# Earlier weight loads, later q and k loads and an earlier U product in a fused attention and mixer kernel

## The chip, the cores and the metric

The kernel runs on one core of a Trainium2 chip. Its time is the device time of one execution in microseconds (us). A core has five engines with an instruction stream each: PE (TensorE, matmuls; its weight loads are shown apart as PEld), DVE (VectorE), ACT (ScalarE), POOL (GpSimd) and SP (SyncE, which here only issues DMAs). Each engine takes its instructions in order. SP and POOL issue DMAs: SP's go to a hardware queue, POOL's to a software queue, and the same 16 DMA engines move both.

## The reference

Batch 4, 8 heads, 768 positions, head size 64; x is then 4 x 768 x 512.

```
scores = q @ k^T / 8 + bias          # bias: -slope_h * distance
keep   = (column < 8) or (0 <= row - column < 96)
a      = softmax(scores where keep)  # others -1e9
x      = (a @ v), heads side by side # (4, 768, 512)
h      = x^T @ U @ V                 # U 768x32, V 32x768: mixes positions
u      = x + h^T
out    = u + relu(u @ w_ch1) @ w_ch2 # 512 -> 2048 -> 512
```

The mask leaves each block of 128 rows its own block of columns, the block before it, and the first 8 columns.

## The kernel before, in words

**Pairs.** The work goes by pairs of heads: pair i is batch i // 4, heads 2 (i % 4) and the next. There are 16. `NP` is 4 and `NPE` is 8. For a pair the steps are: `load_qk` and `load_v` (SP issues the loads of q, k and v in float32), `cast_qk` and `cast_v` (casts to float16, on POOL from pair 3 on), then the turning of q and k, which for pairs below 8 is PE transposes (`st_T`) and for pairs 8 to 15 two DMA transposes that SP issues (`turn`, L323 for k, L326 for q). `st_K` (L335, L336, DVE) or `st_KA` (L290, L291, POOL) makes `kA`, the keys of the block before with the 8 global ones. `st_A` makes `vA` the same way, as a POOL copy (L299) below pair 8 and as DMAs from pair 8 on (L302, L303). `st_S` computes scores on PE (L360, L367) and drains them on DVE with the bias (L392); `st_E` is the exponential on ACT (L404). `st_V` is the product with v on PE (L416, L420); DVE divides (L425, L439) and POOL casts the result to float16 (L440) as `x16`.

**The mixer.** For each pair, `st_M1` multiplies x16 by U on PE (L449; batch 0: L457), DVE copies the result (L453), `st_MT` turns it on PE (L466, drained by L467), `st_M3` multiplies by V (L503) and DVE adds it to x (L508); POOL casts u to float16 (L512), and `st_X` has SP issue a DMA transpose of it (L492), which makes `uT`. Batch 0 uses `st_M2` instead.

**The feed-forward.** It is cut into units: an up unit is 8 matmuls with w1 (L609) and a Relu on ACT (L614); a down unit is 4 matmuls with w2 (L639) and, in the last groups, 8 matmuls with sums of quarters (L659). `fill(n)` runs n units from two queues, so units stand between the attention steps of the pairs as filler for PE. A batch's units are queued (`queue_ff`) when its four pairs are done.

**Weights.** w1 is loaded in four quarters of 512 columns and w2 in four pieces of 512 rows, each by one DMA that POOL issues (`load_w1` L222, `load_w2` L225), which casts to float16 on the way (512 KB written each).

**Order.** All of it is written out by hand: nothing reorders it, and an engine runs its instructions in the order of the program. First comes a loop over pairs 0 to 3, then a stretch that finishes batch 0, then a loop in which iteration i does the attention of pair i, the product with v and the mixer of pair i - 1 and the loads for later pairs. Staging buffers for q and k are two deep.

Of the kernel before, what the change touches and what calls it, by code (L numbers as in the profile page):

```python
# [20 lines left out]
def kernel(  # L21
# [24 lines left out]
    NP = H // 2  # L46
    NPE = 2 * NP
# [38 lines left out]
    def ps_cps(name):  # L86
        return psum.tile([P, 512], FP32, name=name, tag="cps", bufs=2)
# [8 lines left out]
    def load_qk(i, behind=None):  # L96

        b, h0 = i // NP, 2 * (i % NP)
        got = []
        for src, nm in ((q, "qst"), (k, "kst")):  # L100
            st = stp.tile([P, 2, NSB, D], FP32, name=nm, tag=nm, bufs=2)
            if behind is not None:
                behind.memset(st[0:1, 0, 0, 0:1], 0.0)
            if i < NPE:
                nc.sync.dma_start(  # L105
                    st.rearrange("p h n d -> p h (n d)"),
                    src[b, h0:h0 + 2].rearrange("h (p n) d -> p h (n d)", n=NSB),
                )
            else:
                nc.sync.dma_start(  # L110
                    st.rearrange("p h n d -> p (h n) d"),
                    src[b, h0:h0 + 2].rearrange("h (n p) d -> p (h n) d", p=P),
                )
            got.append(st)
        staged[i] = got

    def cast_qk(i, *engs):
        got = []
        for st, nm, eng in zip(staged.pop(i), ("q16", "k16"), engs * 2):
            st16 = stp.tile([P, NSB, 2, D], FP16, name=nm, tag=nm, bufs=2)  # L120
            turn_over = eng.copy if eng is nc.scalar else eng.tensor_copy
            turn_over(st16.rearrange("p n h d -> p h n d"), st)
            got.append(st16)
        cast[i] = got
# [17 lines left out]
    NPAIR = B * NP  # L142
# [77 lines left out]
    def load_w1(c):  # L220
        js = slice(c * (DFF // 4), (c + 1) * (DFF // 4))
        nc.gpsimd.dma_start(w1_16[:, :, js], w1v[:, :, js])  # L222

    def load_w2(c):
        nc.gpsimd.dma_start(w2_16[:, 4 * c:4 * c + 4], w2v[:, 4 * c:4 * c + 4])  # L225
# [85 lines left out]
    def st_P(i):  # L311
        nc.vector.tensor_copy(  # L312
            vas[i][0:NG, 1:].rearrange("p n h d -> p n (h d)"),
            vts[i][0:NG, 0:1].rearrange("p n h d -> p n (h d)").broadcast_to(
                (NG, NSB - 2, 2 * (D + 1))
            ),
        )
# [84 lines left out]
    def st_E(i, hi):  # L402
        ep = scp.tile([P, W], FP16, name=f"ep{hi}", tag=f"ep{hi}")
        nc.scalar.activation(  # L404
            ep, sps.pop((i, hi)), AF.Exp, scale=slope[2 * (i % NP) + hi]
        )
        eps[i, hi] = ep

    def st_V(i, hi):
        b, h = i // NP, 2 * (i % NP) + hi  # L410
        ep, vt, vA = eps.pop((i, hi)), vts[i], vas[i]
        obf = ps_cps("ob") if (i, hi) == (NP - 1, 1) else ps_ob()
        ob = obf[:, 0:NSB * (D + 1)].rearrange("p (n d) -> p n d", n=NSB)
        for qi in range(NSB):
            if qi:
                nc.tensor.matmul(  # L416
                    ob[:, qi], ep[:, OF[qi - 1]:OF[qi - 1] + P], vA[:, qi - 1, hi],
                    start=True, stop=False,
                )
            nc.tensor.matmul(  # L420
                ob[:, qi], ep[:, DG[qi]:DG[qi] + P], vt[:, qi, hi],
                start=(qi == 0), stop=True,
            )
        rcp = vap.tile([P, NSB], FP32, name="rcp", tag="rcp")
        nc.vector.reciprocal(rcp, ob[:, :, D])  # L425
        xo = xs[b][:, :, h * D:(h + 1) * D]
        x16 = x16s[b][:, i % NP, :, hi * D:(hi + 1) * D]
        rb = rcp.unsqueeze(2).broadcast_to((P, NSB, D))
        if i == NP - 1:
            if hi == 1:  # L430
                nc.vector.tensor_tensor(x16, ob[:, :, 0:D], rb, ALU.mult)
            else:
                for n in range(NSB):
                    nc.scalar.activation(
                        x16[:, n], ob[:, n, 0:D], AF.Copy, scale=rcp[:, n:n + 1]
                    )
            later.append((xo, ob[:, :, 0:D], rb))
            return
        nc.vector.tensor_tensor(xo, ob[:, :, 0:D], rb, ALU.mult)  # L439
        nc.gpsimd.tensor_copy(x16, xo)  # L440
# [22 lines left out]
    def st_MT(i):  # L463
        b, dc = i // NP, i % NP
        tps = ps_ob()
        nc.tensor.matmul(tps[:, 0:P], turn16[i % 2], ident16, start=True, stop=True)  # L466
        nc.vector.tensor_copy(tmps[b][:, dc * P:(dc + 1) * P], tps[:, 0:P])  # L467
# [22 lines left out]
    def st_X(i):  # L490
        b, dc = i // NP, i % NP
        nc.sync.dma_start_transpose(  # L492
            uTs[b][:, dc].rearrange("d (n p) -> d n p", n=NSB),
            x16s[b][:, dc].rearrange("p n d -> p (n d)"),
        )
# [195 lines left out]
    def fill(n):  # L691
        for _ in range(n):
            unit()
            if jobs:
                jobs.popleft()()
# [22 lines left out]
    for i in range(NP):  # L718
        st_SE(i, 0)
        if i:  # L720
            st_V(i - 1, 0)
        cast_v(i)
        st_A(i)
        if i < 2:
            load_v(i + 2)
        if i == 0:
            load_uv()
        if i == 1:
            load_qk(NP)
        if i == 2:  # L730
            load_w1(0)
            load_qk(NP + 1, nc.gpsimd)
        if i == 3:
            load_v(NP)
        if i == NP - 1:
            st_M1(i - 2)
        if i:
            st_T(i + 1)
        st_SE(i, 1)
        if i == 2:  # L740
            st_M1(i - 2)
        if i:
            st_V(i - 1, 1)
        else:
            st_T(i + 1)
        st_KA(i + 1, nc.vector)
        st_P(i)
        if i == 0:
            cast_qk(i + 2, nc.vector)
        elif i < 3:  # L750
            cast_qk(i + 2, nc.gpsimd)
        if i == 2:
            load_w1(1)
        st_SE(i, 2)
        if i >= 2:
            st_M2(i - 2)
# [17 lines left out]
    for i in range(NP, NPAIR + 2):  # L774
        b, hp = divmod(i, NP)
        live = i < NPAIR
        units = iter(
            (1, 1, 1, 1, 1, 1, 1, 1, 0) if i + 1 < NPE
            else (1, 1, 1, 2, 1, 1, 1, 1, 1) if i < 2 * NP + 1
            else (2, 1, 1, 2, 1, 1, 1, 1, 1)  # L780
        )
        held[0] = i < NP + 3
        if hp == 0 and live and b + 1 < B:
            new_batch(b + 1)
        if live and i > NP:
            st_S(i, 0)
        if NPE <= i + 1 < NPAIR:
            turn(i + 1)
        if i + 1 < NPAIR:
            load_v(i + 1)  # L790
        if i + 2 < NPE:
            load_qk(i + 2)
        fill(next(units))
        if NP < i <= NPAIR:
            st_V(i - 1, 0)
        if i + 1 < NPE:
            st_T(i + 1)
        if i == NP:
            load_w1(2)
        if live:  # L800
            cast_v(i)
            st_A(i)
            if i == NP:
                load_w1(3)
        fill(next(units))
        if live:
            st_S(i, 1)
        fill(next(units))
        if NP < i <= NPAIR:
            st_V(i - 1, 1)  # L810
        if NPE <= i + 3 < NPAIR:
            load_qk(i + 3)
        if i > NP + 1 and (i - 2) % NP == NP - 1:
            queue_ff((i - 2) // NP)
            ahead[0] = 1
        if i == NPAIR + 1:
            break
        fill(next(units))
        if live:
            st_S(i, 2)  # L820
            if i < NPE:
                st_P(i)
        fill(next(units))
        if i > NP:
            st_M1(i - 1)
        if i == NP + 1:
            load_w2(0)
            load_w2(1)
        if i + 2 < NPE:
            cast_qk(i + 2, nc.gpsimd)  # L830
        if live:
            st_E(i, 0)
        fill(next(units))
        if i > NP:
            st_MT(i - 1)
        if NPE <= i + 1 < NPAIR:
            st_K(i + 1)
        fill(next(units))
        if i > NP:
            st_M3(i - 1, 0)  # L840
        if live:
            st_E(i, 1)
        fill(next(units))
        if i > NP:
            st_M3(i - 1, 1)
            st_X(i - 1)
        if i == NP + 1:
            load_w2(2)
            load_w2(3)
        if NPE <= i + 2 < NPAIR:  # L850
            cast_qk(i + 2, nc.gpsimd)
        fill(next(units))
# [38 lines left out]
```

## Time and profile before

| what | value |
|---|---|
| median of 3 runs | 233.44 us (232.91 to 236.33) |
| the profiled execution: its own time | 232.94 us |
| its span in the profile | 231.0 us |
| PE busy | 223.2 us, 97% of the span |
| DVE, ACT, POOL busy | 152.7, 110.9, 80.5 us |
| granted TensorE clock | 1.0 throughout |
| DMA | 36.66 MB, mean 159 GB/s; the share of the 16 engines is about 0.9 to 1.25 in most stages from 24 to 108 us and below 0.8 afterwards |
| w1 and w2 loads | 8 of 512 KB, median 8.9 us from issue to landing |
| q and k loads | 16 of 384 KB each, median 4.2 and 4.9 us to landing |

The span runs from the first to the last instruction of the program; the 1.9 us beside it lie around the program. The profile's durations are those of one execution. PE's busy time counts matmuls as pipelined, so it is not a measure of how well each is used; what it shows here is where PE has gaps.

### The profile page before, as it was taken

To read this page: it belongs to the slowest core of one execution; us is meant where nothing else is said; L and a number is where in the kernel's file an instruction comes from. 1 tells how busy PE (TensorE), PEld (TensorE's weight loads), DVE (VectorE), ACT (ScalarE), POOL (GpSimd) and SP (SyncE) were. 2 spreads that over 40 slices of the span, in tenths; PEclk is the share of its full clock that TensorE was granted. 3 is DMA by queue.
4 is the path that set the end of the run, shared out by engine and by line. 5 is a ranking of instruction groups with operands and counts; after the bars stand their busy time and mean duration, and the time that the engine had idled before them with its cause. 6 is when DMAs were issued, how large, how long until landed. Compare 5 with 4: busy or idle time off the path is not lost.

```text
span 231.0 us, 5678 instructions
## 1 busy us (share of the span) xinstructions
PE 223.2 (97%) x2324; PEld 161.8 (70%) x2324; DVE 152.7 (66%) x350; ACT 110.9 (48%) x167; POOL 80.5 (35%) x131
## 2 busy tenths in 40 slices
PE   7989999999999999999999999999999999999994
PEld 2455678788644457766666656866688888888883
DVE  3697797868677667566656675779895524444452
ACT  6776957685621313827363707473633334333320
POOL 6399728577444243433424051504120100000000
PEclk9999999999999999999999999999999999999999
DMA  6997998999999999897786955633131302011112
GB/s 183 321 280 201 280 203 188 261 259 175 213 210 244 209 315 216 220 182 188 157 226 134 258 140 145 148 100 79 32 81 48 79 3 91 1 48 45 45 48 91
DMA packets 86561, 36.66 MB, mean 159 GB/s; under 512 B 74152, under 2 KB 83592, under 8 KB 86536
## 3 DMA queue, kind: packets, MB, share of 16 engines
q1 hardware_dynamic: 81480, 32.01, 55.1%
q0 software_dynamic: 5056, 4.29, 12.3%
q8 instruction: 18, 0.29, 0.5%
q14 instruction: 7, 0.06, 0.1%
HBM read 27.46 MB, written 6.29 MB: 146 GB/s over the span
## 4 chain that ended last, share of the span: by engine, by line
PE 86%; POOL 3%; DMA 3%; ACT 3%; DVE 2%; issue 1%; SPq 1%; POOLq 0%
PE hps L609 35%; PE cps L639 22%; PE cx L659 8%; PE cy L659 5%; PE sc L360 4%; DMA vst<-in_v_dram 3%; PE ob L420 2%; PE ob L416 2%; PE sc L367 2%; ACT htr L614 1%; ACT ep L404 1%; PE tp L250 1%; PE sc L503 1%; PE ob L503 1%; SPq L105 1%
## 5 line engine op out<-in xcount | busy, mean ns | idle before, releaser
L614 ACT ACTIVATE htr<-hps 128x512 f16<-128x512 f32 x96 | 56.6, 598 | 85.0 <-PE hps L609 82.2
L609 PE MATMUL hps<-uT,w 128*128 128x256 f16 x756 | 96.2, 273 | 0.5 <-DVE uT L485 0.3
L609 PEld LDWEIGHTS <-w 128*128 128x128 f16 x756 | 70.5, 98 | 11.3 <-issue 0.4
L639 PE MATMUL cps<-w,htr 128*128 128x512 f16 x224 | 56.9, 379 | 0.0
L392 DVE SCALAR_TENSOR_TENSOR sp<-sc,relcat 128x512 f32<-128x512 f32 (+1 forms) x72 | 43.3, 641 | 15.5 <-PE sc L360 8.9
L404 ACT ACTIVATE ep<-sp 128x1408 f16<-128x1408 f32 x24 | 32.8, 1374 | 16.3 <-DVE sp L392 16.3
L512 POOL CAST x<-x_sb 128x768 f16<-128x768 f32 x12 | 10.3, 856 | 60.5 <-DVE x_sb L508 60.5
L639 PEld LDWEIGHTS <-htr 128*128 128x128 f16 x224 | 19.1, 97 | 16.6
L440 POOL CAST x<-x_sb 128x384 f16<-128x384 f32 x30 | 15.8, 525 | 26.8 <-DVE x_sb L439 26.7
L360 PEld LDWEIGHTS <-kT 64*128 64x128 f16 x192 | 8.2, 93 | 15.1 <-issue 13.5
L540 DVE TENSOR_TENSOR s<-htr 128x512 f16<-128x512 f16 x20 | 9.3, 464 | 12.7 <-ACT htr L614 12.7
L439 DVE TENSOR_TENSOR x_sb<-ob,rcp 128x384 f32<-128x384 f32 x30 | 16.7, 558 | 1.0
L659 PEld LDWEIGHTS <-s 128*128 128x128 f16 x160 | 15.5, 98 | 1.8
L360 PE MATMUL sc<-qT,kT 64*128 64x128 f16 x192 | 16.7, 221 | 0.0
L420 PE MATMUL ob<-v,ep 128*128 128x65 f16 x192 | 16.2, 193 | 0.0
L420 PEld LDWEIGHTS <-ep 128*128 128x128 f16 x192 | 13.8, 98 | 2.7 <-ACT ep L379 0.3
L664 DVE TENSOR_TENSOR x_sb<-cx,x_sb 128x256 f32<-128x256 f32 x20 | 8.5, 423 | 10.1 <-PE cx L659 10.0
L136 POOL CAST v<-vst 128x768 f16<-128x768 f32 x16 | 13.4, 839 | 4.5 <-DMA vst<-in_v_dram 4.5
L367 PE MATMUL sc<-qT,kA 64*128 64x128 f16 x160 | 14.1, 216 | 0.9 <-DVE kA L286 0.9
L379 ACT ACTIVATE ep<-sc 128x512 f16<-128x512 f32 (+1 forms) x24 | 12.0, 559 | 5.1 <-PE sc L367 4.8
L416 PE MATMUL ob<-vA,ep 128*128 128x65 f16 x160 | 14.3, 194 | 0.2 <-DVE vA L312 0.2
L659 PEld LDWEIGHTS <-htr 128*128 128x128 f16 x120 | 11.7, 98 | 1.3
(102 smaller groups left out, 269.4 us busy)
## 6 DMA issues: line engine op xcount, KB each, us to landing
qst<-in_q_dram SPq DMA_DIRECT2D x16, 384.0 KB, 4.2
kst<-in_k_dram SPq DMA_DIRECT2D x16, 384.0 KB, 4.9
vst<-in_v_dram SPq DMA_DIRECT2D x16, 384.0 KB, 3.4
out_dram<-x_sb SPq DMA_DIRECT2D x23, 256.0 KB, 2.3
w<-in_moe_w_ch_dram POOLq DMA_DIRECT2D x8, 512.0 KB, 8.9
vA<-v SPq DMA_DIRECT2D x8, 152.3 KB, 4.3
out_dram<-x_sb SPq DMA_DIRECT2D x2, 128.0 KB, 1.7
uT<-x SPq DMA_TRANSPOSE x12, 2.8
```

The lines of the kernel that those rows point to most:

```text
L360: nc.tensor.matmul(scs[hi][:, o:o + P], kT[r, kb * P:(kb + 1) * P], qT[r, kb * P:(kb + 1) * P], start=(o == 0 and not on_pe), stop=(o + P ...
L367: nc.tensor.matmul(scs[hi][:, o + P:o + 2 * P], kA[r, kb], qT[r, (kb + 1) * P:(kb + 2) * P], start=False, stop=(o + 2 * P == tot),)
L392: nc.vector.scalar_tensor_tensor(out=dst, in0=got, scalar=qk_scale / slope[2 * (i % NP) + hi], in1=relfs[c0 // 512], op0=ALU.mult, op1=ALU ...
L404: nc.scalar.activation(ep, sps.pop((i, hi)), AF.Exp, scale=slope[2 * (i % NP) + hi])
L416: nc.tensor.matmul(ob[:, qi], ep[:, OF[qi - 1]:OF[qi - 1] + P], vA[:, qi - 1, hi], start=True, stop=False,)
L420: nc.tensor.matmul(ob[:, qi], ep[:, DG[qi]:DG[qi] + P], vt[:, qi, hi], start=(qi == 0), stop=True,)
L439: nc.vector.tensor_tensor(xo, ob[:, :, 0:D], rb, ALU.mult)
L440: nc.gpsimd.tensor_copy(x16, xo)
L609: nc.tensor.matmul(hps[:, k * FT:(k + 1) * FT], w1_16[:, dc, jt * P:(jt + 1) * P], uT[:, dc, ts], start=(dc == 0 and k == 0), stop=(dc == ...
L614: nc.scalar.activation(cell["htr"][:, 2 * jp:2 * jp + 2].rearrange("p j t -> p (j t)"), hps, AF.Relu)
L639: nc.tensor.matmul(cps, htr[:, jc, t * P:(t + 1) * P], w2_16[:, jc], start=(b > 0 and jc == 0), stop=(jc == NJC - 1),)
L659: nc.tensor.matmul(ps, cell[a][:, j], tw[w][:, j], start=(first and j == 0), stop=(done is not None and j == HJ - 1), skip_group_check=True,)
```

## The change

It moves instructions and adds none.

- w1's first quarter is issued in iteration 1 of the first loop, behind the casts of pair 3's q and k, instead of in iteration 2.
- w1's third quarter is issued in iteration 4 before `st_T(5)` and with it the POOL copies of kA, instead of behind them; the fourth takes the third's old place, ahead of the cast of v.
- w2's first piece is issued in iteration 5 ahead of the cast of v, instead of behind the U product of that iteration.
- `load_qk(i + 3)`, in iterations 5 to 12 (pairs 8 to 15), goes from the middle of the iteration to a place behind `st_X(i - 1)`. On SP's queue it then stands before `turn(i + 2)`, the next v and the next vA, which stood before it.
- In iteration 8, M1, MT, M3 and the x transpose of pair 7 are each one unit earlier.

```diff
         if i == 2:
-            load_w1(0)
             load_qk(NP + 1, nc.gpsimd)
...
+        if i == 1:
+            load_w1(0)
         if i == 2:
             load_w1(1)
...
+        if i == NP:
+            load_w1(2)
         if i + 1 < NPE:
             st_T(i + 1)
         if i == NP:
-            load_w1(2)
+            load_w1(3)
+        if i == NP + 1:
+            load_w2(0)
         if live:
             cast_v(i)
             st_A(i)
-            if i == NP:
-                load_w1(3)
...
-        if NPE <= i + 3 < NPAIR:
-            load_qk(i + 3)
...
+        if i == NPE:
+            st_M1(i - 1)
         fill(next(units))
-        if i > NP:
+        if i > NP and i != NPE:
             st_M1(i - 1)
         if i == NP + 1:
-            load_w2(0)
             load_w2(1)
...
         if live:
             st_E(i, 0)
+        if i == NPE:
+            st_MT(i - 1)
         fill(next(units))
-        if i > NP:
+        if i == NPE:
+            st_M3(i - 1, 0)
+        elif i > NP:
             st_MT(i - 1)
         if NPE <= i + 1 < NPAIR:
             st_K(i + 1)
-        fill(next(units))
-        if i > NP:
+        if i == NPE:
+            fill(next(units))
+            st_M3(i - 1, 1)
+            st_X(i - 1)
+        else:
+            fill(next(units))
+        if i > NP and i != NPE:
             st_M3(i - 1, 0)
         if live:
             st_E(i, 1)
         fill(next(units))
-        if i > NP:
+        if i > NP and i != NPE:
             st_M3(i - 1, 1)
             st_X(i - 1)
+        if NPE <= i + 3 < NPAIR:
+            load_qk(i + 3)
```

## Prediction

> **What bounds the kernel now.** I read the page first, then the table by stage, then the order of instructions on PE, DVE, POOL and SP around every instruction that the change moves.
>
> From the page: span, PE's row, PE in 40 slices, the chain that ended last.
>
> ```profile
> span 231.0 us, 5678 instructions
> ...
> PE 223.2 (97%) x2324; PEld 161.8 (70%) x2324; DVE 152.7 (66%) x350; ACT 110.9 (48%) x167; POOL 80.5 (35%) x131
> ...
> PE   7989999999999999999999999999999999999994
> ...
> PE 86%; POOL 3%; DMA 3%; ACT 3%; DVE 2%; issue 1%; SPq 1%; POOLq 0%
> ```
>
> PE is busy 97% of the span and makes up 86% of the chain. Its idle time is 231.0 - 223.2 = 7.8 us, nearly all of it before 36 us and after the last matmul. Five stages of the table by stage show it (length, then busy us of PE, PEld, DVE, ACT, POOL, granted clock, DMA share, GB/s):
>
> ```profile
> 30.00:36.00 6.00, 5.52 (x68) 4.40 (x65) 4.97 (x9) 3.06 (x7) 1.92 (x5) 1.00 0.89 204
> 36.00:42.00 6.00, 5.92 (x74) 5.04 (x71) 4.88 (x6) 5.35 (x8) 3.80 (x5) 1.00 1.02 200
> 48.00:54.00 6.00, 6.00 (x83) 5.10 (x81) 4.38 (x9) 5.53 (x8) 4.74 (x8) 1.00 1.25 231
> 60.00:66.00 6.00, 6.00 (x63) 3.15 (x61) 4.99 (x10) 1.78 (x3) 4.00 (x6) 1.00 1.22 244
> 102.00:108.00 6.00, 5.95 (x55) 3.85 (x54) 3.63 (x9) 4.08 (x5) 0.33 (x2) 1.00 1.04 257
> ```
>
> From 42 us on PE has no gap to give, at full clock. The change acts from 18 to about 135 us. PE's idle time there, by the same table, is 0.26 (18 to 24 us) + 0.29 + 0.48 + 0.08 (to 42 us) + 0.05 (102 to 108 us) = 1.2 us: the most that earlier loads could win. No PE wait in the table of waits names w1, w2 or uT of a later batch; PE's one wait on a uT (0.3 us, DVE L485) is on batch 0's drain. The loads that are hastened are not waited for. So the question is what the moves delay.
>
> **The change, part by part.** It adds and removes no work: the built order has the same matmuls, casts and transfers on each engine. Each part is priced by what it pushes back.
>
> (1) w1's first quarter. Now POOL issues it at 20.53 us (0.79 us); it lands 5.4 us later, at 26.0, and PE first reads it at 29.36 (L523): 3.4 us early already, so no gain. Moved behind pair 3's k cast (17.73 + 0.82 = 18.55), it pushes the x cast L440 (18.51, 0.50), pair 2's v cast and its vA copy back by 0.75 us. That x cast is the last input of M1(0), on PE at 19.82: the cast ends at 19.01 now, 19.78 then, and a wait for POOL ends some 0.05 us later on PE (row: cast end 17.79, tp at 17.84). Price 0 to 0.1 us. The vA copy then ends at 21.35; its reader L312 starts at 21.66, so nothing more.
>
> (2) w1's third and fourth quarter. They are issued at 35.20 and 37.52 now, behind the kA copies, for which POOL idles 4.02 us; then at 30.24 and about 35.2. They land at 42.2 and 48.1 now and are first read at about 46 and 54 us (13th and 19th up unit): no gain. POOL's work up to pair 6's casts is the same sum. The third quarter's 512 KB now run before pair 6's q and k, which land at 38.0; k's cast starts at 39.02 and ends at 39.86, and PE transposes k at 41.74, so 38.0 may slip 2.9 us before PE waits. One quarter lasts 2.6 us at 200 KB per us, the rate of the software queue's packets when alone (51 to 54 us). Price 0, at most 0.3.
>
> (3) w2's first piece. It is read at 60.80 and lands at 54.0 now: no gain. But it moves in front of pair 5's v cast. The timeline of POOL there, and PE's reader:
>
> ```profile
> 44.34 0.21 POOL L291 COPY kA<-kT 128x32 f16<-128x32 f16 x1
> 44.49 0.84 POOL L136 CAST v<-vst 128x768 f16<-128x768 f32 x1
> 45.39 0.73 POOL L299 COPY vA<-v 128x650 f16<-128x650 f16 x1
> 46.07 0.51 POOL L440 CAST x<-x_sb 128x384 f16<-128x384 f32 x1
> 46.52 1.48 POOL L225 DMA_DIRECT2D w<-in_moe_w_ch_dram  x2
> 46.87 0.30 PE L449 MATMUL ob<-u,x 128*128 128x32 f16 x6
> ```
>
> Its issue costs POOL 1.48/2 = 0.74 us, so the x cast L440 ends at 46.58 + 0.74 = 47.32. M1(4), the last row, needs that cast and runs at 46.87: it waits until about 47.4. Price 0.5 us, on PE's path, in a stage with nothing to absorb it.
>
> (4) Pair 7's U product a unit sooner. M1(7) comes before a down unit instead of behind it: 78.34 instead of 79.21. Its x16 is cast by 77.81, so it starts at once. The next step does not move up by as much: DVE's copy L453 stands behind two L392 (78.44 + 1.02 = 79.46) and ends at 79.64, while PE finishes the one unit between (0.30 + 0.86 us) by about 79.4. In the rows of before L453 ends at 80.20 and MT(7) starts at 80.44, so MT would start at 79.64 + 0.24 = 79.88. Price 0.4 to 0.5 us of PE waiting; the bound below is 0, if the scores' drains come sooner. X(7) leaves about 1 us sooner, for a read at 88.80 that is not waiting (it lands at 87.7 now): no gain.
>
> (5) Pairs 8 to 15 loaded behind the turn of x. In each of these iterations q and k (384 KB each) now stand on SP before kT and qT of the pair ahead, v and vA, instead of behind them. One iteration of before, SP's issues (start, duration) and the first readers of kT:
>
> ```profile
> 96.55 1.25 SPq L492 DMA_TRANSPOSE uT<-x  x1
> 98.09 1.29 SPq L323 DMA_TRANSPOSE kT<-k  x1
> 99.44 1.29 SPq L326 DMA_TRANSPOSE qT<-q  x1
> 100.78 0.58 SPq L129 DMA_DIRECT2D vst<-in_v_dram  x1
> 101.46 0.90 SPq L302 DMA_DIRECT2D vA<-v  x1
> ...
> 103.21 0.45 SPq L110 DMA_DIRECT2D qst<-in_q_dram  x1
> 103.71 1.37 SPq L110 DMA_DIRECT2D kst<-in_k_dram  x1
> ...
> 105.70 0.32 DVE L335 COPY kA<-kT 128x640 f16<-128x640 f16 x1
> ...
> 108.00 0.23 PE L360 MATMUL sc<-qT,kT 64*128 64x128 f16 x2
> ```
>
> Moved, q and k are issued at 97.85 and end their issue near 99.75 (0.45 + 1.37 us). Now k lands 108.46 - 103.21 = 5.25 us after q's issue; then 103.1. kT, lined up behind, lands about 1.2 us later (an issue's length), 104.3; qT 105.5, v 107.3, vA 107.8. Needed: kT at 105.70 (DVE) and, through kA, at 108.00 (PE); qT at 108.00; vA at 110.08. The least slack is 1.4 us. Price 0. The thin place is the start: pair 8's load goes from 39.45 to 53.1, while its cast stands on POOL at 61.82 and 62.59. In front of it are the transposed x (192 KB), and beside it two w2 pieces (1 MB, 5.2 us at 200 KB per us) and then v. Since w1 and w2's first half are done sooner by then, I work out 192 + 768 KB at 260 KB per us (63 to 66 us) = 3.7 us, plus 5.2, from 53.3: about 62.2. Price 0 to 0.8 us, and 0.85 us of M1(6)'s slack behind it (x cast ends 66.85, M1 at 67.69). I take 0.
>
> Sum: 0.1 + 0 + 0.5 + 0.5 + 0 = +1.1 us; span 232.1, and 232.94 + 1.1 = 234.0 for an execution like the profiled one (its span and 1.9 us around it). The median of the runs shown is 233.44, 0.5 above the profiled one; I name 234.3, between the two. Bounds: all stalls 0 and 1.2 us won is 231.7; all upper prices, +2.5, is 236.
>
> **Rivals.**
>
> Pair 8 caught behind the flood of w2, slower. For: pair 9's q, issued at 53.83 beside w2, landed 12.2 us later; in 57 to 61 us the trace's packets show some 152 KB per us on the software queue and 36 to 41 on SP's. If w2 is no faster through, pair 8's halves take the places of the landings after x's at 62.0: 64.7 and 66.0, and v 67.9. Then POOL casts k until 66.9, v until 68.8, copies vA until 69.6, casts x until 70.1, and M1(6) starts at 70.2 instead of 67.7: +2.5 on top of +1.1, so 236.8. It decides once k lands after about 63.4. Against: with pair 8's 768 KB out of 39 to 51 us, w2's first half should be through by 53.
>
> [...]
>
> The turns late in every iteration, slower by over 2%. If kT and qT behind q and k lose as much as x did at 74.08 (landed 78.1, 4.0 us), in sequence, then kT lands at 107.1 and vA near 111, 0.9 us after PE needs it; seven turns stand behind loads, so about +0.9 x 6 = 5.4: 239.5. Against: the 1.4 us of slack above; DMA share falls to 0.76 after 108 us.
>
> Faster inside the noise: the waits of (3) and (4) don't show and the early fills win their 1.2 us: 232.2. Faster by over 2% (4.7 us) has no place in PE's rows.
>
> **How the numbers follow.** Forecast 68%, flood 13%, late turns 9%, slightly faster 7%, unseen losses over 2% 2%, unseen gains over 2% 1%. 2% (4.7 us, under 228.8 or over 238.1) is about what a measurement of this kernel tells from no change. Slower over 2%: 9 + 2, some 3 of the flood's and 1 of the forecast's upper ends, 15%; faster 2%, the unseen gains and a little of the slightly faster; within 83%. The range reaches from the slightly faster case to past the flood: 232.2 to 237.6.
>
> **What would show it.** Right: M1(4) waits on POOL's L440 near 47 us, MT(7) on DVE's L453 near 80, each some 0.5 us; PE 6.00 of 6.00 after 84 us; L335 without a wait on kT. Wrong: PE idle at every score stage from 96 us (late turns), a POOL wait on qst or kst at 62 to 66 us with PE idle at 68 (flood), or a span under 230.

## The result, and the profile after

| what | before | after |
|---|---|---|
| median of the runs timed together | 233.96 us (22 runs) | 235.48 us (22 runs) |
| ratio after / before | | 1.0079 (95% interval 1.0054 to 1.0105) |
| profiled execution: its own time, its span | 232.94, 231.0 us | 236.74, 234.9 us |
| PE busy | 223.2 us | 224.1 us |

The ratio makes the change slower by 0.0079 x 234 = 1.85 us (1.3 to 2.5). Executions of the kernel before scatter from 232 to over 240 us, so medians of different sets are not compared with each other, and ratios leave out executions more than 1.5% above the fastest of their kernel. The profiled execution of after lies 1.3 us above its median and that of before 0.5 to 1.0 below its medians, so the two profiles differ by more (3.9 us of span) than the kernels do.

The page of after: span, PE's row, PE in 40 slices, the chain that ended last.

```profile
span 234.9 us, 5670 instructions
...
PE 224.1 (95%) x2323; PEld 161.4 (69%) x2324; DVE 151.2 (64%) x350; ACT 111.3 (47%) x167; POOL 80.3 (34%) x131
...
PE   7889999999969999999999999999999999999994
...
PE 73%; DMA 9%; POOL 5%; DVE 4%; SPq 4%; ACT 2%; issue 1%; POOLq 0%
```

The twelfth slice fell from 9 to 6; it runs from 11 x 234.9 / 40 = 64.6 to 70.5 us. The chain now runs through DMA for 9% instead of 3%, and through PE for 73% instead of 86%. PE's idle time grew from 7.8 to 234.9 - 224.1 = 10.8 us.

The table by stage of after (length, then busy us of PE, PEld, DVE, ACT, POOL, granted clock, DMA share, GB/s):

```profile
30.00:36.00 6.00, 5.52 (x65) 4.53 (x62) 5.27 (x10) 3.22 (x6) 2.11 (x5) 1.00 1.19 282
36.00:42.00 6.00, 5.97 (x73) 4.96 (x72) 3.05 (x5) 5.19 (x8) 3.42 (x5) 1.00 1.17 212
42.00:48.00 6.00, 5.62 (x71) 4.28 (x71) 5.16 (x11) 3.58 (x7) 4.53 (x8) 1.00 0.63 156
48.00:54.00 6.00, 6.00 (x78) 5.28 (x76) 3.96 (x9) 5.47 (x7) 4.16 (x7) 1.00 0.91 147
54.00:60.00 6.00, 6.00 (x78) 5.02 (x77) 4.01 (x10) 3.78 (x6) 3.33 (x6) 1.00 1.19 134
60.00:66.00 6.00, 6.00 (x68) 3.52 (x66) 4.80 (x10) 2.60 (x4) 1.74 (x3) 1.00 1.25 246
66.00:72.00 6.00, 3.72 (x28) 1.52 (x27) 2.77 (x6) 2.64 (x2) 3.21 (x5) 1.00 1.41 210
...
102.00:108.00 6.00, 6.00 (x75) 4.07 (x71) 3.84 (x9) 1.36 (x3) 2.45 (x4) 1.00 1.15 219
```

Two of these stages in the kernel before:

```profile
42.00:48.00 6.00, 6.00 (x78) 4.84 (x76) 4.84 (x11) 3.59 (x7) 4.83 (x9) 1.00 1.16 272
...
66.00:72.00 6.00, 6.00 (x45) 2.79 (x43) 3.98 (x11) 2.65 (x2) 0.92 (x3) 1.00 0.97 181
```

PE was busy 6.00 of 6.00 in both. Now 0.38 us is lost in the one and 2.28 us in the other, 2.66 of the 3.0 us that PE's idle time grew by. One line of after's table of waits (engine and line, releaser, us in total, times, longest) names both:

```profile
PE ob L449 <- POOL x L440: 2.6, 2, 2.3
```

L449 is M1. It waits twice for POOL's cast L440: at M1(4), as forecast, and at M1(6), which was a rival. The timeline of POOL and PE at M1(4) in after:

```profile
44.79 0.74 POOL L225 DMA_DIRECT2D w<-in_moe_w_ch_dram  x1
45.53 0.85 POOL L136 CAST v<-vst 128x768 f16<-128x768 f32 x1
46.30 1.05 PE L609 MATMUL hps<-uT,w 128*128 128x256 f16 x8
46.44 0.73 POOL L299 COPY vA<-v 128x650 f16<-128x650 f16 x1
47.11 0.51 POOL L440 CAST x<-x_sb 128x384 f16<-128x384 f32 x1
...
47.67 0.32 PE L449 MATMUL ob<-u,x 128*128 128x32 f16 x6 [0.33 <-POOL x L440]
```

w2's first piece (L225) now stands ahead of the v cast, and PE waits 0.33 us for the x cast at the end of that queue. The bracket gives the idle time and what ended it. Idle time counts from the modelled end of the matmul before, so it is less than what is lost. By starts, M1(4) comes 1.37 us behind the start of the unit before it (46.30 to 47.67) instead of 0.88 (45.99 to 46.87): 0.5 us later.

The timeline of POOL in after where the large wait arises:

```profile
61.86 0.83 POOL L512 CAST x<-x_sb 128x768 f16<-128x768 f32 x1 [4.40 <-DVE x_sb L508]
64.51 0.83 POOL L122 CAST q<-qst 128x768 f16<-128x768 f32 x1 [1.83 <-DMA qst<-in_q_dram]
65.92 0.83 POOL L122 CAST k<-kst 128x768 f16<-128x768 f32 x1 [0.58 <-DMA kst<-in_k_dram]
66.69 0.51 POOL L440 CAST x<-x_sb 128x384 f16<-128x384 f32 x1
68.81 0.84 POOL L136 CAST v<-vst 128x768 f16<-128x768 f32 x1 [1.61 <-DMA vst<-in_v_dram]
69.70 0.73 POOL L299 COPY vA<-v 128x650 f16<-128x650 f16 x1
70.38 0.51 POOL L440 CAST x<-x_sb 128x384 f16<-128x384 f32 x1
```

POOL waits for pair 8's q, then its k, then v: 1.83 + 0.58 + 1.61 = 4.0 us. The last x cast ends at 70.89 instead of 66.85. It, the unit before M1(6) and M1(6), in before and then PE's two in after:

```profile
66.34 0.51 POOL L440 CAST x<-x_sb 128x384 f16<-128x384 f32 x1
66.81 1.04 PE L639 MATMUL cps<-w,htr 128*128 128x512 f16 x4
67.69 0.31 PE L449 MATMUL ob<-u,x 128*128 128x32 f16 x6
```

```profile
67.63 1.04 PE L639 MATMUL cps<-w,htr 128*128 128x512 f16 x4
70.94 0.32 PE L449 MATMUL ob<-u,x 128*128 128x32 f16 x6 [2.28 <-POOL x L440]
```

M1(6) starts 3.31 us behind the unit before it instead of 0.88, 2.4 us later. Why the data are late is seen on SP's queue in after (start and length of each issue):

```profile
52.59 1.31 SPq L492 DMA_TRANSPOSE uT<-x  x1
53.95 0.57 SPq L110 DMA_DIRECT2D qst<-in_q_dram  x1
54.63 5.36 SPq L110 DMA_DIRECT2D kst<-in_k_dram  x1
60.03 3.94 SPq L129 DMA_DIRECT2D vst<-in_v_dram  x1
```

The x transpose of pair 4 is at the head. It is issued at 52.59, as w2's third and fourth piece are (52.5 and 53.2), and by the trace lands at 62.0; the pieces land at 60.0 and 63.3. Pair 8's q lands at 64.5, its k at 65.9, v at 68.8.

MT(7) is the third place, and a small one. PE's timeline there in before, then the chain that ended last in after (start and length of each piece):

```profile
79.58 1.02 PE L639 MATMUL cps<-w,htr 128*128 128x512 f16 x4
80.44 0.22 PE L466 MATMUL ob<-ident,zw 128*128 128x128 f16 x1
```

```profile
82.01 1.01 DVE sp L392 x2
83.02 0.11 DVE zw L453
83.13 0.05 issue
83.18 0.23 PE ob L466
```

In after the unit before MT(7) starts at 82.06 and MT(7) at 83.18: 1.12 us behind it instead of 0.86, so 0.26 us later. Only 0.09 us of this is idle time. The line "PE ob L466 <- DVE zw L453: 0.2, 1, 0.2" in the table of waits isn't this place: it is in before's table too, at 176.46 us.

### The profile page after: what moved, and what is told of

The parts are those of the page before. It is cut to its first block, busy times and chain, and to the rows that moved or that the text cites. A ratio compares the mean times of both kernels' runs of the same rounds, so it can differ in the third digit from the quotient of the medians.

```text
span 234.9 us, 5670 instructions
## 1 busy us (share of the span) xinstructions
PE 224.1 (95%) x2323; PEld 161.4 (69%) x2324; DVE 151.2 (64%) x350; ACT 111.3 (47%) x167; POOL 80.3 (34%) x131
## 4 chain that ended last, share of the span: by engine, by line
PE 73%; DMA 9%; POOL 5%; DVE 4%; SPq 4%; ACT 2%; issue 1%; POOLq 0%
PE hps L609 29%; PE cps L639 17%; PE cx L659 7%; DMA vst<-in_v_dram 7%; PE cy L659 5%; PE sc L360 3%; SPq L110 3%; DMA kT<-k 2%; PE ob L420 2%; PE ob L416 2%; PE sc L367 1%; ACT ep L404 1%; POOL v L136 1%; ACT htr L614 1%; SPq L105 1%
## 5 line engine op out<-in xcount | busy, mean ns | idle before, releaser
L609 PE MATMUL hps<-uT,w 128*128 128x256 f16 x756 | 96.2, 273 | 0.5 <-DVE uT L485 0.3
L609 PEld LDWEIGHTS <-w 128*128 128x128 f16 x756 | 70.5, 98 | 11.3 <-issue 0.4
L639 PE MATMUL cps<-w,htr 128*128 128x512 f16 x224 | 56.8, 379 | 0.0
L639 PEld LDWEIGHTS <-htr 128*128 128x128 f16 x224 | 19.2, 97 | 16.6
L440 POOL CAST x<-x_sb 128x384 f16<-128x384 f32 x30 | 15.7, 524 | 26.8 <-DVE x_sb L439 26.7
```

The lines of the kernel that those rows point to most:

```text
L609: nc.tensor.matmul(hps[:, k * FT:(k + 1) * FT], w1_16[:, dc, jt * P:(jt + 1) * P], uT[:, dc, ts], start=(dc == 0 and k == 0), stop=(dc == ...
L639: nc.tensor.matmul(cps, htr[:, jc, t * P:(t + 1) * P], w2_16[:, jc], start=(b > 0 and jc == 0), stop=(jc == NJC - 1),)
```

## The experiments

They ran in three sets, each set on one chip together with the kernel before. "After" or "before" says which kernel an edit starts from. Times from issue to landing are from the traces.

**Pair 8 alone put back.** In after, pair 8's load goes ahead of the x transpose of pair 4; pairs 9 to 15 stay behind theirs.

```diff
+        if i + 3 == NPE:
+            load_qk(i + 3)
         if i > NP and i != NPE:
             st_M3(i - 1, 1)
             st_X(i - 1)
-        if NPE <= i + 3 < NPAIR:
+        if NPE < i + 3 < NPAIR:
             load_qk(i + 3)
```

> The change, but pair 8's q and k load stands on SP ahead of the turn of x of pair 4, as before; pairs 9 to 15 stay behind it. Flood theory (pair 8's load, held behind that turn, is caught beside w2's last two pieces, and M1(6) waits for POOL): PE's wait on L440 near 68 us (2.3 us in the profile after) vanishes, the waits of M1(4) (0.5 us) and MT(7) (0.3 us) stay; about 1.003 of before. Late turns (pairs 9 to 15): stays at 1.008. Early weights (w1 and w2 sooner crowd SP's queue): pair 8 still lands late and the wait stays.

Ratio 0.9996 (0.9970 to 1.0021), span 231.1 us: the loss is gone, and the ratio is below the 1.003 that was expected, which had no gain of w1 in it. Pair 8's k lands at 47.2 us. The table of waits of this kernel has L449 once:

```profile
PE ob L449 <- POOL x L440: 0.3, 1, 0.3
```

M1(4) still waits, and MT(7) for 0.09 us; M1(6) does not.

**Pair 8 alone moved.** Before, with only pair 8's load behind the x transpose.

```diff
-        if NPE <= i + 3 < NPAIR:
+        if NPE < i + 3 < NPAIR:
             load_qk(i + 3)
...
             st_X(i - 1)
+        if i + 3 == NPE:
+            load_qk(i + 3)
```

> The kernel before, with pair 8's q and k load alone moved behind the turn of x of pair 4. Flood theory: M1(6) waits for L440 again, and longer than the 2.3 us of the profile after, since w2's first half is not hastened here: 2.5 to 4 us, 1.011 to 1.017. Late turns: no difference, 1.000. Early weights: no difference, since the weights are where they were.

Ratio 1.0127 (1.0070 to 1.0183): this one move makes a loss of the size of the whole change's or more (the intervals overlap). k lands at 65.1 us. PE's timeline in this kernel:

```profile
66.82 1.04 PE L639 MATMUL cps<-w,htr 128*128 128x512 f16 x4
70.30 0.34 PE L449 MATMUL ob<-u,x 128*128 128x32 f16 x6 [2.45 <-POOL x L440]
70.48 1.87 PE L639 MATMUL cps<-w,htr 128*128 128x512 f16 x4
...
72.25 1.57 PE L639 MATMUL cps<-w,htr 128*128 128x512 f16 x4
...
74.03 1.03 PE L639 MATMUL cps<-w,htr 128*128 128x512 f16 x4
```

The same wait, 2.45 us (M1(5) waits 0.34 us too). Then the same four matmuls take 1.87 and 1.57 us instead of 1.03: the granted clock is 0.83 from 66 to 72 us and 0.89 from 72 to 78. Counted from start to start, that is (72.14 - 70.48) + (73.65 - 72.25) = 3.06 us where two units of 0.86 stood, 1.3 us more (72.14 and 73.65 are the starts of the rows left out behind each).

**Pairs 9 to 15 alone moved.** Before, with only their loads behind the turns of x.

```diff
-        if NPE <= i + 3 < NPAIR:
+        if i + 3 == NPE:
             load_qk(i + 3)
...
             st_X(i - 1)
+        if NPE < i + 3 < NPAIR:
+            load_qk(i + 3)
```

> The kernel before, with the q and k loads of pairs 9 to 15 alone moved behind the turn of x. Flood theory: no difference, 0.998 to 1.002, no PE wait on kT, qT or vA, though kT lands later than before by 2 us or more. Late turns: the whole 1.008, as PE waits at scores from 96 us on.

Ratio 0.9978 (0.9937 to 1.0018). DVE's kA copy L335 waits for kT three times (1.46, 0.81 and 0.17 us), and PE never waits for it. The rival of late turns in every iteration falls.

**w2's first piece alone.** Before, with load_w2(0) ahead of the v cast of iteration 5.

```diff
+        if i == NP + 1:
+            load_w2(0)
         if live:
             cast_v(i)
...
         if i == NP + 1:
-            load_w2(0)
             load_w2(1)
```

> The kernel before, with w2's first piece alone issued ahead of pair 5's v cast. Theory of the POOL queue: M1(4) waits 0.5 us for L440 near 47 us and nothing else changes, 1.002. Rival (the earlier piece clears the flood and wins something): 0.998 or less. The other rival (it crowds SP's loads): a POOL or PE wait at 48 to 52 us and over 1.004.

Ratio 1.0018 (0.9976 to 1.0060). The wait of 0.3 us at M1(4) is there (0.5 us by starts); the interval holds both 0 and the 0.5 us that was forecast. That profile also has waits that nothing in the edit explains (PE for qT 0.6 us, for uT 0.4 us).

**The U product alone.** Before, with the four places of iteration 8 as in after.

```diff
+        if i == NPE:
+            st_M1(i - 1)
         fill(next(units))
-        if i > NP:
+        if i > NP and i != NPE:
             st_M1(i - 1)
...
```

> The kernel before, with pair 7's U product alone one unit sooner. Theory: MT(7) waits for DVE's L453 by 0.25 to 0.5 us near 80 us, nothing else; 1.001 to 1.002. Rival (the sooner turn of x of pair 7 wins at the first units of batch 1): PE excess falls near 89 us and the ratio is 0.998 or less.

Ratio 0.9980 (0.9947 to 1.0014), and MT(7) waits for DVE's L453: 0.09 us of idle time, 0.26 us by starts as in after. No cost shows in the times.

**After, with the x transpose behind pair 8's load.** The x transpose of pair 4 moves into iteration 6, behind the next v. Pair 8's load keeps its late start: a POOL memset of one element of each staging buffer holds it until 52.2 us.

```diff
+        if i == NP + 2:
+            st_X(i - 2)
         if i + 2 < NPE:
             load_qk(i + 2)
...
             st_M3(i - 1, 1)
-            st_X(i - 1)
-        if NPE <= i + 3 < NPAIR:
+            if i > NP + 1:
+                st_X(i - 1)
+        if i == NP + 1:
+            load_qk(i + 3, nc.gpsimd)
+        elif NPE < i + 3 < NPAIR:
             load_qk(i + 3)
```

> The change, with pair 8's q and k load still held back to the end of iteration 5 (by a one-element POOL memset in each staging buffer, behind the cast L512 of pair 4), but with the turn of x of pair 4 behind it and behind pair 7's v on SP. So pair 8 is as late in issue (about 52.6 us) and has w2's third and fourth piece beside it, but not the x transpose ahead of it. If the w2 pieces alone starve pair 8: k lands at 64 to 66 us as in the profile after (65.9) and M1(6) waits 2 us or more, 1.008. If it is the x transpose at the head of SP's queue (10 us to land beside w2): k lands by 59 us, no wait at M1(6), 1.000 to 1.003.

Ratio 1.0028 (1.0001 to 1.0054): between the two theories. q lands at 59.3 instead of 64.5 us, v at 65.0 instead of 68.8, but k at 63.7, only 2.2 us sooner. M1(6) no longer waits. The head of SP's queue is thus part of the delay; w2 beside the load is the other part. Instead PE loses 0.93 us between 72 and 78 us, at pair 8's scores, to DVE's L508 and to qT.

**After, with w2's last two pieces issued sooner**, right behind the second, at 47 us instead of 52.5.

```diff
         if i == NP + 1:
             load_w2(1)
+            load_w2(2)
+            load_w2(3)
...
-        if i == NP + 1:
-            load_w2(2)
-            load_w2(3)
```

> The change, with w2's third and fourth piece issued right behind the second (about 47.6 us instead of 52.5), into the stage in which the profile after shows a DMA share of 0.63. If the x transpose and pair 8 are slow because two w2 pieces run beside them: w2 is done by 56 to 58 us, the x transpose lands by 58, pair 8's k by 62, and M1(6) waits less than 0.5 us; about 1.003, with the waits of M1(4) and MT(7). If the lateness of pair 8's issue alone does it: k still lands after 65 and M1(6) still waits over 2 us. Its own risk: POOL's casts of pair 7 are 1.5 us later, which PE's transposes near 52 us would show as 0 to 0.5 us.

Ratio 0.9981 (0.9951 to 1.0011), span 231.0 us, no wait at M1(6). The pieces land at 55.9 and 59.6, x at 60.1, k at 62.6, each some 2 us or less behind what was expected. Pair 8 may start late, if w2 ends 3.7 us sooner. With the run before, the wait at M1(6) needs both: the x transpose ahead of the load, and w2's end as late as 63.3.

**w1 alone.** Before, with only the three quarters of w1 sooner.

```diff
-            load_w1(0)
...
+        if i == 1:
+            load_w1(0)
...
+        if i == NP:
+            load_w1(2)
...
         if i == NP:
-            load_w1(2)
+            load_w1(3)
...
-            if i == NP:
-                load_w1(3)
```

> The kernel before, with w1's first, third and fourth quarter alone sooner. Theory: nothing waits for them, 0.999 to 1.001, at most 0.1 us at M1(0) near 20 us; pair 6's k may land up to 1.5 us later without a PE wait. Rival (it crowds pair 6's loads): PE waits at the transposes near 41 us, over 1.002. Rival (it clears the queue for later loads): 0.998 or less.

Ratio 0.9938 (0.9903 to 0.9973), span 230.1 us: faster than both kernels, where steps (1) and (2) had priced no gain. The span says little of it: PE's first L609 starts at 31.3 us here, at 32.1 in before and at 31.5 in a copy of before, and its last at 220.4 instead of 221.3, so the profile is ahead by 0.8 us from the start and hardly more at the end. None of its 12 executions was above 233.95 us; the 35 of before that ran with it went from 233.13 to 240.61.

**The same kernel again, and a copy of before**, to see whether that holds.

> The kernel before with w1's first, third and fourth quarter alone sooner, a second time, beside a copy of the kernel before that is timed the same way. If the first result (0.9938) is a gain from w1: 0.992 to 0.996 again, and 1 us or more under the copy's median. If it came of the state of the chip and of the runs of before that it was compared with: 0.997 to 1.001, and within 0.5 us of the copy.

> The kernel before, unchanged, timed as if it were a change: what the measurement shows where there is no difference. 0.998 to 1.002 if the comparison is sound; below 0.997 if the runs of before are systematically the slower ones in it, and then the ratios of the other small edits are to be read against this one.

w1 alone: 0.9864 (0.9779 to 0.9950), span 230.3 us, a larger gain than the 0.992 to 0.996 that were expected. The copy: 1.0007 (0.9955 to 1.0059). The gain holds, and the comparison itself is even. The copy's profiled execution took 238.55 us, and its table of waits has a line that no other profile here has, PE L639 waiting for w2's DMA, 3.1 us in two. PE's timeline and the table by stage in that execution of the unchanged kernel:

```profile
61.33 1.02 PE L639 MATMUL cps<-w,htr 128*128 128x512 f16 x4
64.56 1.59 PE L639 MATMUL cps<-w,htr 128*128 128x512 f16 x4 [1.88 <-DMA w<-in_moe_w_ch_dram]
67.94 1.86 PE L639 MATMUL cps<-w,htr 128*128 128x512 f16 x4 [1.19 <-DMA w<-in_moe_w_ch_dram]
...
70.03 1.86 PE L639 MATMUL cps<-w,htr 128*128 128x512 f16 x4
```

```profile
60.00:66.00 6.00, 4.12 (x33) 1.90 (x33) 3.47 (x7) 1.10 (x2) 2.88 (x4) 0.91 1.01 134
66.00:72.00 6.00, 4.81 (x27) 1.95 (x25) 1.45 (x3) 0.00 (x0) 2.02 (x3) 0.53 0.97 208
72.00:78.00 6.00, 6.00 (x50) 2.95 (x45) 3.95 (x11) 2.64 (x2) 0.80 (x2) 1.00 0.90 181
```

The third piece of w2 lands at 64.5 us and the fourth at 67.9, and PE stands before each. From start to start the three units shown last take 1.38 + 1.66 + 1.79 us at the lower clock instead of 0.87 each, 2.2 us more (their next starts are 65.94, 69.60 and 71.82). This span is 236.4 us, 5.4 above that of the profile of before, and up to 62 us this execution was 0.7 us ahead of it, so some 6 us are lost behind that, of which 3.1 + 2.2 = 5.3 are these. Whether the executions nearer the copy's median (235.5 us) hold a smaller wait of this kind is not shown.

**w1 and all of w2 sooner.** The kernel with w1 alone, with w2's last two pieces behind the second as well.

> The kernel before with w1 sooner and all four pieces of w2 issued in one place in iteration 5 (46 us), pair 8's load where it was. A candidate for beating both kernels: no PE wait is added (w2 first stays behind the x cast that M1(4) needs), and the load of pair 9 and the x transposes land sooner. By the theory that PE has nothing to win after 42 us: within 0.2% of the w1 kernel. Risk: POOL's casts of pair 7 1.5 us later, 0 to 0.5 us at PE's transposes near 52 us.

Ratio 0.9886 (0.9821 to 0.9951), span 231.7 us, against 0.9864 and 230.3 us for w1 alone in the same set: nothing more is won.

**After, with w2's first piece put back** behind the U product.

> The change, with w2's first piece back behind the x cast that M1(4) needs. POOL queue theory: M1(4)'s wait on L440 near 47 us (0.5 us) is gone; M1(6)'s wait near 68 us stays, and is the same or up to 1 us longer since w2's first piece is 2 us later; 1.006 to 1.010. If w2's first piece matters for the flood: 1.010 or more, M1(6) waits 3 us or more.

Ratio 1.0032 (0.9982 to 1.0082). M1(4)'s wait is gone, M1(6)'s is 2.1 us, MT(7)'s stays. The ratio is under the 1.006 to 1.010 expected, but the interval holds them, and the difference to after is within the intervals.

## Why the prediction was right and where it was not

The time was right: 235.48 us measured beside a before of 233.96, and +1.85 us by the ratio, inside the range, against +1.1. The sum was not. It missed a loss and a gain that partly cancel, so that the time came out so near was in part luck.

**Step (5), the failed one.** "I take 0" stood on k of pair 8 landing at about 62.2 us. It landed at 65.9, past the 63.4 that the text itself named as the point of decision, and the flood rival (13%) happened, with the rows it gave: v's cast until 69.65 (forecast 68.8), the x cast until 70.89 (70.1), M1(6) at 70.94 (70.2), PE idle for 2.28 us (2.5). The two experiments on pair 8's place show it from both sides: moved alone it gives 1.0127, and with it put back the ratio is 0.9996. The error is in two terms. The estimate let 960 KB through at 260 KB per us; that is about the rate of 63 to 66 us in the profile of before (276 GB/s), where w2 was through (63.5). With w2's 1,024 KB it makes 1,984 KB in 8.9 us, 228 GB/s. In after the DMA engines moved 179 GB/s from 53.3 to 65.9 us, and 134 from 54 to 60 us. And it held that w2's first half being through by 53 us would end the flood sooner. The first half was through (53.4 us, 3.2 sooner than before), but the second half did not follow: it is issued from 52.5 us on in after, from 51.7 in before, and lands at 60.0 and 63.3 against 60.2 and 63.5. Between them the x transpose takes from 52.6 to 62.0 us, where the median of its kind is 2.8 us, much as in before (51.8 to 62.0). The prediction had the rows for it, that landing and the 36 to 41 KB per us on SP's queue beside w2's 152, and put it to the rival instead of the sum.

How the two queues shared the DMA engines is seen in one stretch: from 57 to 61 us the profile of before has 619 packets of the software queue and 610 of SP's, 0.62 and 0.16 MB, and that of after 478 and 480, 0.47 and 0.12 MB: about as many packets, and a fifth of the bytes for SP's queue, in both. When w2 ends does not decide by itself whether M1(6) waits: the fourth piece outlasts 60 us in after (63.3, k at 65.9) and no piece does where they are issued sooner (59.6, k at 62.6), but with the x transpose behind pair 8 the fourth lands at 62.8 and M1(6) does not wait.

**Steps (1) and (2), a gain priced at nothing.** "The hastened loads are not waited for" was true of the one execution that the profile showed. There w2's third and fourth piece landed at 60.23 and 63.52 us and were read at 63.29 and 64.50: 3.1 and 1.0 us of margin. In the copy's profiled execution they came after PE. With w1 sooner alone they land at 57.9 and 61.3 and are read at 62.5 and 63.7: 4.5 and 2.4 us. So with w1 sooner both pieces have 1.4 us more margin.

The other runs fit this. Where w1 and pair 8's load stand as before, the fourth piece has 0.5 to 1.0 us of margin in the profiles of before, of pairs 9 to 15, of w2's first piece and of the U product alone, and none in that of the copy. Of these three edits' and the copy's executions 14 of 48 took 236 us or more, and 41 of the 110 of before beside them. In the six runs with w1 sooner and no wait at M1(6) the margin is 2.0 to 4.7 us, and 1 of 60 executions took as long; within each of the three sets the order is the same. The idle PE that the prediction counted as the most to win is not where this comes from: in 18 to 42 us w1 alone has only the 0.26 us of 18 to 24 us less of it, and the copy of before lacks these too. That the move gains is shown (0.9938 and 0.9864); that it gains by this margin is read from these rows and not isolated by a run of its own. M1(0)'s price of 0 to 0.1 us was 0: it starts some 0.15 us behind the score matmuls before it in after (19.99 to 20.14) as in before (19.66 to 19.82).

**Step (3)**, M1(4) waiting for POOL's L440 near 47 us: right, in size too. By starts it is 0.5 us; the idle time is 0.33 us in PE's row and 0.38 us in the stage. **Step (4)**, MT(7) waiting for DVE's L453: right in kind, at 83.18 us in after (the forecast said near 80, without the losses before it). It is 0.26 us by starts, not 0.4 to 0.5. The forecast put MT(7) 0.24 us behind the end of L453, from rows of before where PE was not waiting for it; in after it starts 0.06 us behind (82.94 + 0.18 = 83.12 against 83.18). Neither is resolved by the ratio of its own run. Of the bounds, the upper prices add up to 0.1 + 0.3 + 0.5 + 0.5 + 0.8 = 2.2 us and not 2.5.

**The steady state of step (5)** was right in its result: PE is at 6.00 of 6.00 in 102 to 108 us, pairs 9 to 15 alone cost nothing. One sign was not as forecast. L335 was to have no wait for kT, and in after it waits 1.41, 0.45 and 1.57 us in its first three iterations and none from 109 us on. The slack of 1.4 us was also too large for the iteration that stands for the one worked out: kT lands at 109.61 us, 2.3 us behind k instead of 1.2, and DVE copies it at 109.65. PE's scores follow at 111.95, so the cover was PE's later need and not the 1.4 us.

Put together from the measured parts, by starts: 0.5 (M1(4)) + 2.4 (M1(6)) + 0.3 (MT(7)) + 0.3 (pair 8's scores, where PE starts behind DVE's L508 at 75.6 us) = 3.5 us, and -1.4 for w1 (0.0062 x 234, itself -2.3 to -0.6): +2.1, against the measured 1.3 to 2.5. The two profiles lie 3.9 us apart because to the 3.5 us come 0.3 us that after loses at the start (its first L609 is at 32.5 us, that of before at 32.1), and the profile of before is one in which w2 was in time. The clock after the wait may add to it in some executions. After's profile does not show it (1.00 in 66 to 78 us), that of pair 8 alone does (0.83 and 0.89). The four executions of after above 237 us, up to 238.6, had a mean granted clock of 0.990 to 0.993 and the others 0.998 to 1.000, which would fit; no trace of one of them was taken.

## What to carry to other kernels

When a load is moved behind a transfer, price the transfer that will then stand at the head of its queue beside whatever else runs at that hour (here 9.4 us, where the median is 2.8), with that stretch's own rate, and not the load by its median. A load that is "not waited for" in one profile still has a margin: read landing against first use, and where it is 1 us, look at the scatter of the times before pricing a gain at nothing. Here the parts of one change went both ways, and the part that had no wait to its name (w1 sooner, alone) is the version to keep.

## What the runs showed of the hardware

An x transpose issued on SP's queue beside two 512 KB weight pieces on the software queue took 9.4 us (52.6 to 62.0) where the median is 2.8, and pair 8's q, issued behind it on SP's queue at 53.95, landed at 64.5, 10.5 us later. With q ahead of the transpose on that queue it was 7.1 us (issued at 52.2, landed at 59.3).

Gaps of PE were followed by a lower granted clock in some executions: 0.53 from 66 to 72 us behind gaps of 1.88 and 1.19 us (before's copy), 0.83 and 0.89 behind one of 2.45 us (pair 8 alone), the four matmuls of a unit taking 1.86 us instead of 1.03, and the copy's units 1.66 and 1.79 us from start to start instead of 0.87. Behind gaps of 2.28 us in after and 2.1 us in after with w2's first piece put back it stayed at 1.00 (66 to 78 us). So behind a wait of 2.45 us the units took 1.3 us more, and behind two of 3.1 us together 2.2 more, but not behind every wait: those of 2.28 and 2.1 us were followed by none.
